# Moving the transposes of B and C from TensorE to the DMA from pair 4 on

## The chip, the cores and the metric

The kernel runs on one core of one Trainium2 chip. The metric is the time of one execution in microseconds on the device; the profile's span of the same execution is some 1.75 us shorter. Most repeated runs of one kernel agree within about 1%, and a run that is over 1.5% above the fastest of its kernel is called slow and left out of ratios.

## The reference, cut to what matters

A Mamba-2 style scan in chunks feeds a bilinear feed-forward layer: 4 batches, 8 heads, 768 positions, head dimension 32, state dimension 16; 3072 tokens of 256 features, 1536 hidden.

```python
for c in range(nc):                      # the reference uses chunks of 32; the kernel uses 128
    cum = np.cumsum(la, axis=-1)
    L = np.exp(cum[:, :, :, None] - cum[:, :, None, :]) * causal
    CB = np.einsum('bhin,bhjn->bhij', Cc, Bc)          # scores: contract over n
    y_intra = np.einsum('bhij,bhjd->bhid', CB * L, xc)
    y_inter = np.einsum('bhin,bhnd->bhid', Cc, state) * decay_to_i[:, :, :, None]
    ...                                                # state update
x = y.transpose(0, 2, 1, 3).reshape(B * S, H * D)
out = ((x @ w_a) * (x @ w_b)) @ w_out
```

The scores contract over n, so B and C, which arrive with positions on partitions, have to be transposed.

## The kernel before

A pair is two batches of one block of 128 positions; there are 12. A partition holds two neighbouring positions (i, r), r = 0 or 1. The loop from pair 4 on mixes the scan of pair p with the feed-forward of pairs p-1 and p-2:

```python
    def transposes(p, ps=None):
        ...
        for T_, src in ((TB, s["bm"]), (TC, s["cm"])):
            for r in range(2):
                nc.tensor.transpose(T_[:, r * 128 : (r + 1) * 128], src[:, r]..., ident)
        for e in range(2):                       # ScalarE, with the odd or even heads zeroed
            nc.scalar.activation(out=BT[:, e]..., in_=TB, func=AF.Copy, scale=par[:, e : e + 1])
        (nc.scalar.copy ...)(CT.rearrange("p t (i r) -> p r (t i)", r=2), TC...)   # natural order

    for p in range(4, NP):
        scores(p)                                # reads BT, CT of pair p
        if p + 1 < NP: scale(p + 1)              # GpSimd: B, C, x of the next pair
        if p + 2 < NP: load(p + 2)               # SyncE: six loads
        ...                                      # units (p - 1, 0..2) and masks
        out_half(p - 2, 0)                       # 12 matmuls, eviction, one store on SyncE
        go((p - 1, 3)); pull(p); pv(p); state(p)
        if p + 1 < NP: transposes(p + 1)
        out_half(p - 2, 1)
        ...
        go((p - 1, 4), (p - 1, 5))
```

Each engine runs its instructions in the written order; SyncE issues loads and stores in that order too.

## Time and profile before

| | before |
|---|---|
| time, median of 3 runs | 132.21 us (131.5 to 132.58) |
| span of the profiled run | 130.4 us |
| TensorE, VectorE, ScalarE, GpSimd busy | 93, 66, 57, 41% |
| scores of pair 4 start | 41.38 us |
| one pass of the loop, scores to scores | 9.38 us |

The last two rows come from the timeline of TensorE: the start of the first of 32 small matmuls (L279) marks each pass. Ends of matmuls are modelled and starts are not. The scores of pairs 4 to 6:

```profile
41.38 0.43 PE L279 MATMUL SC<-ct,bt 32*64 32x128 f16 x32
...
51.11 0.43 PE L279 MATMUL SC<-ct,bt 32*64 32x128 f16 x32
...
60.49 0.43 PE L279 MATMUL SC<-ct,bt 32*64 32x128 f16 x32
```

The stores of the kernel before, by tensor (durations of the issue in ns: least, median, most):

```profile
L454 SPq DMA_DIRECT2D out_dram<-osb x23: 332/338/570, 29.8 to 127.3; - x23
```

### The profile page before, as it was taken

What the parts mean: (1) busy time and instruction counts of PE and PEld (TensorE: products, weight loads), DVE (VectorE), ACT (ScalarE), POOL (GpSimd) and SP (SyncE); (2) the same over time, 40 slices, a digit from 0 to 9 for tenths busy, and PEclk for the clock granted to TensorE, in tenths of its full rate; (3) what the DMA queues carried; (4) which work ended last, traced back from release to release, by engine and by line L of the source; (5) the groups of instructions that cost most, each with busy time, mean ns of one, the idle gap of its engine ahead of it and who ended that gap; (6) DMA issues with size and microseconds to landing.
All of it is one profiled execution on the core that took longest, in us unless ns stands there. A gap on an engine that the chain in (4) does not pass through costs nothing.

```text
span 130.4 us, 4718 instructions
## 1 busy us (share of the span) xinstructions
PE 121.3 (93%) x1947; PEld 100.3 (77%) x1947; DVE 86.4 (66%) x163; ACT 74.9 (57%) x154; POOL 53.2 (41%) x72
## 2 busy tenths in 40 slices
PE   6959879988999999999999999999999999999980
PEld 2326758876888888888988888898888888888870
DVE  2676579592683975965966948948939829744440
ACT  3345576864647566576475576575486485464520
POOL 7787531943975808309219129037056000000000
PEclk9999999999999999999999999999999999999999
DMA  3999999047667452532623344514510110110102
GB/s 70 158 204 200 209 207 188 17 70 159 113 130 183 78 139 58 106 80 65 115 71 81 66 104 85 116 45 98 113 59 22 45 40 5 40 40 5 59 21 80
DMA packets 44805, 12.22 MB, mean 94 GB/s; under 512 B 38576, under 2 KB 44752, under 8 KB 44784
## 3 DMA queue, kind: packets, MB, share of 16 engines
q1 hardware_dynamic: 39264, 9.08, 33.1%
q0 software_dynamic: 3216, 2.36, 12.2%
q10 hardware_dynamic: 2304, 0.48, 1.8%
q8 instruction: 15, 0.25, 0.8%
q14 instruction: 6, 0.05, 0.2%
HBM read 11.13 MB, written 3.15 MB: 109 GB/s over the span
## 4 chain that ended last, share of the span: by engine, by line
PE 69%; DMA 19%; SPq 2%; DVE 2%; POOL 2%; ACT 1%; issue 1%; ACTq 1%; POOLq 0%; DVEq 0%
PE ops L437 22%; PE aps L420 19%; PE bps L420 19%; DMA Wo<-in_moe_w_out_dram 9%; DMA bn<-in_B_dram 5%; DMA cn<-in_C_dram 5%; PE SC L321 2%; PE SC L279 2%; PE SC L258 2%; SPq L122 2%; PE SC L355 2%; PE SC L338 1%; DVE hk L430 1%; POOL bm L240 1%; POOL cm L240 1%
## 5 line engine op out<-in xcount | busy, mean ns | idle before, releaser
L430 DVE TENSOR_TENSOR hk<-bps,asb 128x512 f16<-128x512 f32 x72 | 49.0, 687 | 25.0 <-ACT asb L429 24.1
L429 ACT COPY asb<-aps 128x512 f32<-128x512 f32 x72 | 41.9, 588 | 17.1 <-PE aps L420 15.6
L420 PE MATMUL bps<-X2T,Wb 128*128 128x256 f16 x288 | 43.2, 273 | 0.8 <-DMA Wb<-in_moe_w_b_dram 0.7
L420 PE MATMUL aps<-X2T,Wa 128*128 128x256 f16 x288 | 43.5, 273 | 0.0
L437 PE MATMUL ops<-Wo,hk 128*128 128x256 f16 x288 | 35.2, 273 | 0.0
L420 PEld LDWEIGHTS <-Wb 128*128 128x128 f16 x288 | 28.0, 98 | 4.7 <-DMA Wb<-in_moe_w_b_dram 1.0
L312 DVE TENSOR_TENSOR t<-SC,causal 128x512 f16<-128x512 f32 x45 | 29.4, 681 | 2.3 <-ACT tmp L309 2.0
L437 PEld LDWEIGHTS <-hk 128*128 128x128 f16 x288 | 27.7, 98 | 3.2
L420 PEld LDWEIGHTS <-Wa 128*128 128x128 f16 x288 | 26.8, 98 | 4.3 <-DVE X2T L379 0.3
L395 POOL TENSOR_TENSOR sbd<-U,maskbd 128x512 f16<-128x512 f32 x10 | 11.6, 1158 | 31.8 <-DVE U L391 31.7
L452 ACT ACTIVATE osb<-ops 128x256 f32<-128x256 f32 x23 | 8.8, 383 | 18.6 <-PE ops L437 18.6
L234 POOL TENSOR_SCALAR x<-xn 128x512 f16<-128x512 f32 x9 | 13.4, 1490 | 2.4 <-DMA xn<-in_x_dram 1.8
L367 ACT ACTIVATE X2T<-SC 128x512 f16<-128x512 f32 x11 | 6.6, 597 | 7.7 <-PE SC L338 6.7
L240 POOL TENSOR_TENSOR cm<-cn,fC 128x256 f16<-128x256 f32 x11 | 6.8, 619 | 7.4 <-DMA cn<-in_C_dram 7.3
L265 ACT ACTIVATE bt<-SC,ch 128x256 f16<-128x256 f16 x22 | 9.2, 471 | 0.7 <-PE SC L258 0.6
L391 DVE SCALAR_TENSOR_TENSOR U<-SC,G,gU 128x64 f32<-128x64 f32 x16 | 3.8, 280 | 6.4 <-ACT X2T L367 6.4
L240 POOL TENSOR_TENSOR bm<-bn,fB 128x256 f16<-128x256 f32 x11 | 6.9, 626 | 0.0
L279 PEld LDWEIGHTS <-bt 32*64 32x64 f16 x384 | 3.4, 104 | 3.2 <-issue 2.3
L279 PE MATMUL SC<-ct,bt 32*64 32x128 f16 x384 | 5.1, 220 | 0.7 <-ACT ct L266 0.4
L321 PEld LDWEIGHTS <-x 64*32 64x32 f16 x384 | 3.3, 90 | 3.2 <-ACT x L232 1.8
L186 PE MATMUL SC<-warm 128*128 128x512 f16 (+1 forms) x11 | 4.3, 545 | 1.2 <-DVE warm L149 1.2
L266 ACT COPY ct<-SC 128x256 f16<-128x256 f16 x11 | 5.0, 454 | 0.0
(59 smaller groups left out, 68.4 us busy)
## 6 DMA issues: line engine op xcount, KB each, us to landing
xn<-in_x_dram SPq DMA_DIRECT2D x23, 128.0 KB, 3.3
out_dram<-osb SPq DMA_DIRECT2D x23, 128.0 KB, 1.7
bn<-in_B_dram SPq DMA_DIRECT2D x23, 64.0 KB, 2.8
cn<-in_C_dram SPq DMA_DIRECT2D x22, 64.0 KB, 3.0
Wa<-in_moe_w_a_dram POOLq DMA_DIRECT2D x3, 256.0 KB, 6.3
Wb<-in_moe_w_b_dram POOLq DMA_DIRECT2D x3, 256.0 KB, 7.0
Wo<-in_moe_w_out_dram POOLq DMA_DIRECT2D x1, 768.0 KB, 11.9
cn<-in_C_dram ACTq DMA_DIRECT2D x2, 64.0 KB, 5.4
```

Source lines behind the costliest of these rows:

```text
L234: eng.tensor_scalar(xo, xi, XS, None, ALU.mult)
L240: eng.tensor_tensor(out=m_, in0=pair_in[p][which].rearrange("p h r n -> p r h n"), in1=f[:, blk, :, bp].unsqueeze(3).broadcast_to((128, 2, ...
L265: nc.scalar.activation(out=o_, in_=TB, func=AF.Copy, scale=par[:, e : e + 1])
L279: nc.tensor.matmul(SC[m][64 * bt : 64 * bt + 64, c0 : c0 + Q], BT[rows, e, r, bt], CT[rows, bt], start=True, stop=True, skip_group_check=True,
L312: nc.vector.tensor_tensor(out=o_, in0=i_, in1=c_, op=ALU.mult)
L367: nc.scalar.activation(out=X2T[:, p].rearrange("p u t q -> p t u q"), in_=SC1[:, :, 0:256].rearrange("p t (u q) -> p t u q", u=2), func=AF ...
L395: nc.gpsimd.tensor_tensor(out=Sbd.rearrange("p t (m c) -> p t m c", m=4), in0=U32[:, p].unsqueeze(2).broadcast_to((128, 2, 4, 2 * D)), in1 ...
L420: nc.tensor.matmul(ps[:, kk * 2 * Q : (kk + 1) * 2 * Q], W[:, f, k * 128 : (k + 1) * 128], X2T[:, p, f].rearrange("p t q -> p (t q)"), sta ...
L429: nc.scalar.copy(asb, a_ps)
L430: return lambda: nc.vector.tensor_tensor(out=s["hk"][:, 2 * k2 : 2 * k2 + 2, :].rearrange("p k q -> p (k q)"), in0=b_ps, in1=asb, op=ALU.mult)
L437: nc.tensor.matmul(o_ps[:, 0:d_model], hk[:, k, bt * Q : (bt + 1) * Q], Wo[:, k, :], start=(k == 0), stop=(k == NK - 1), skip_group_check= ...
L452: nc.scalar.activation(out=o_sb, in_=o_ps[:, 0:d_model], func=AF.Copy, scale=1.0 / (YS * YS))
```

## The change

The intent is to free TensorE of four transposes a pair and ScalarE of three evictions, with one DMA that transposes 128x768 elements from a tile of six planes (B of even heads, B of odd heads, C, each for r = 0 and 1; the zeros of the B planes are written once at the start). The DMA's output keeps queries in the order (r, i), so the causal mask changes, and each store of 128 rows becomes two of 64, each with every second row. Cut to its core:

```diff
+    bc = [big.tile([128, 6, H, N], f16, name=f"bc{i}") for i in range(2)]
+    bcT = [big.tile([128, 6, 2, 64], f16, name=f"bcT{i}") for i in range(2)]
...
+    DMA_T = 4
+    def scale_planes(p):                 # GpSimd: C planes once, B planes in two halves
+        ...
+    def dma_transposes(p):
+        o_ = bcT[p % 2]
+        nc.sync.dma_start(
+            o_.rearrange("p k t i -> p k (t i)"), bc[p % 2].rearrange("p k h n -> p (k h n)"), transpose=True
+        )
...
-            CT.rearrange("p t (i r) -> p r (t i)", r=2), TC.rearrange("p (r c) -> p r c", r=2)
+            CT.rearrange("p r t i -> p (r t i)"), TC
...
-        (q or nc.sync).dma_start(out[r0 : r0 + Q, :], o_sb)
+        dst = out[r0 : r0 + Q, :].rearrange("(i r) d -> r i d", r=2)
+        for r in range(2):
+            (q or (nc.sync, nc.sync))[r].dma_start(dst[r], o_sb[64 * r : 64 * r + 64])
...
     out_half(1, 1)
+    dma_transposes(4)
     pull(3)
     pv(3)
     state(3)
-    transposes(4)
...
         out_half(p - 2, 0)
+        if p + 1 < NP:
+            dma_transposes(p + 1)
         go((p - 1, 3))
         pull(p)
         pv(p)
         state(p)
-        if p + 1 < NP:
-            transposes(p + 1)
         out_half(p - 2, 1)
```

More of the change, by code (lines that the diff above doesn't have):

```diff
@@ L150 @@
     nc.vector.memset(zero, 0.0)
+    for t_ in bc:
+        nc.vector.memset(t_[:, 0:4].rearrange("p k h n -> p (k h n)").bitcast(u32), 0)
     nc.gpsimd.memset(sel, 1.0)
@@ L176 @@
     for bt in range(2):
-        v = causal[64 * bt : 64 * bt + 64]
+        v = causal[64 * bt : 64 * bt + 64].rearrange("p r (s i) -> p r s i", s=2)
         nc.gpsimd.affine_select(
-            out=v, in_=v, compare_op=ALU.is_ge, fill=0.0, base=0, pattern=[[-1, 2], [1, Q]], channel_multiplier=-2
+            out=v, in_=v, compare_op=ALU.is_ge, fill=0.0, base=0, pattern=[[-1, 2], [1, 2], [2, 64]], channel_multiplier=-2
         )
@@ L246, in scale_bc @@
         st.setdefault(p, {})[name] = m_
-    def scale(p):
+    DMA_T = 4
+    def scale_planes(p):
+        blk, bp = divmod(p, NBP)
+        bn, cn = (pair_in[p][w].rearrange("p h r n -> p r h n") for w in range(2))
+        c_ = bc[p % 2]
+        nc.gpsimd.tensor_tensor(
+            out=c_[:, 4:6], in0=cn, in1=fC[:, blk, :, bp].unsqueeze(3).broadcast_to((128, 2, H, N)), op=ALU.mult
+        )
+        for e in range(2):
+            nc.gpsimd.tensor_tensor(
+                out=c_[:, 2 * e : 2 * e + 2].rearrange("p r (m e) n -> p r m e n", e=2)[:, :, :, e],
+                in0=bn.rearrange("p r (m e) n -> p r m e n", e=2)[:, :, :, e],
+                in1=fB[:, blk, :, bp]
+                .rearrange("p r (m e) -> p r m e", e=2)[:, :, :, e]
+                .unsqueeze(3)
+                .broadcast_to((128, 2, H // 2, N)),
+                op=ALU.mult,
+            )
+    def dma_transposes(p):
+        o_ = bcT[p % 2]
+        nc.sync.dma_start(
+            o_.rearrange("p k t i -> p k (t i)"), bc[p % 2].rearrange("p k h n -> p (k h n)"), transpose=True
+        )
+        st[p]["BT"] = o_[:, 0:4].rearrange("p (e r) t i -> p e r t i", e=2)
+        st[p]["CT"] = o_[:, 4:6]
+    def scale(p):
+        if p >= DMA_T:
+            scale_planes(p)
+            scale_bc(p, 0, nc.gpsimd)
+            scale_x(p, nc.gpsimd)
+            return
         scale_bc(p, 1, nc.gpsimd)
@@ L261, in transposes @@
         BT = mid.tile([128, 2, 2, 2, 64], f16, name="bt", tag="bt")
-        CT = mid.tile([128, 2, Q], f16, name="ct", tag="ct")
+        CT = mid.tile([128, 2, 2, 64], f16, name="ct", tag="ct")
         for e in range(2):
@@ L281, in scores @@
                             BT[rows, e, r, bt],
-                            CT[rows, bt],
+                            CT[rows, :, bt],
                             start=True,
@@ L357, in pv @@
                         s["Sbd"][:, bt, u * 128 : u * 128 + 128],
-                        s["CT"][:, bt],
+                        s["CT"][:, :, bt],
                         start=(u == 0),
@@ L633 @@
         out_mm(NP - 1, bt, o[bt], range(NK - 2, NK))
-        out_store(NP - 1, bt, o[bt], on_dve=bt == 1, q=nc.scalar if bt == 0 else nc.sync)
+        out_store(NP - 1, bt, o[bt], on_dve=bt == 1, q=(nc.scalar, nc.sync))
 _INS = ['x', 'a', 'B', 'C', 'moe_w_a', 'moe_w_b', 'moe_w_out']
```

## The prediction

> **What bounds the kernel now.** I read the page first: busy shares, then the chain of work that ended last, then the groups.
>
> ```profile
> PE 121.3 (93%) x1947; PEld 100.3 (77%) x1947; DVE 86.4 (66%) x163; ACT 74.9 (57%) x154; POOL 53.2 (41%) x72
> ...
> PEclk9999999999999999999999999999999999999999
> ...
> PE 69%; DMA 19%; SPq 2%; DVE 2%; POOL 2%; ACT 1%; issue 1%; ACTq 1%; POOLq 0%; DVEq 0%
> ...
> L265 ACT ACTIVATE bt<-SC,ch 128x256 f16<-128x256 f16 x22 | 9.2, 471 | 0.7 <-PE SC L258 0.6
> L258 PE MATMUL SC<-ident,bm 128*128 128x128 f16 x22 | 3.1, 224 | 0.6 <-POOL bm L240 0.6
> ...
> L266 ACT COPY ct<-SC 128x256 f16<-128x256 f16 x11 | 5.0, 454 | 0.0
> ```
>
> TensorE is busy 93% of 130.4 us, at full granted clock everywhere, and carries 69% of the chain; the 19% of DMA lie before 32 us, while weights and first inputs arrive. ScalarE, whose evictions the change removes (L265, L266), is busy 57% and names no wait of TensorE in the steady part. I then took the busy time by stretches, one loop pass each: the pass from 60.56 to 69.95 us has TensorE busy 9.39 of 9.39 us. So from about 45 us a pass costs what TensorE's instructions cost, and nothing else.
>
> What an instruction is worth there is not its duration, because matmuls overlap. The timeline of TensorE in that pass shows start times:
>
> ```profile
> 63.48 1.47 PE L437 MATMUL ops<-Wo,hk 128*128 128x256 f16 x12
> ...
> 66.49 0.29 PE L258 MATMUL SC<-ident,bm 128*128 128x128 f16 x2
> 66.61 0.27 PE L258 MATMUL SC<-ident,cm 128*128 128x128 f16 x2
> 66.73 1.47 PE L437 MATMUL ops<-Wo,hk 128*128 128x256 f16 x12
> ...
> 69.88 0.32 PE L279 MATMUL SC<-ct,bt 32*64 32x128 f16 x16
> ```
>
> The four transposes of a pair occupy 66.49 to 66.73: 0.24 us, not 4 x 224 ns. The scores of the next pair (L279, their first reader) start at 69.88, over 3 us later.
>
> The other queue that matters is SyncE's, because every new DMA goes onto it in program order. Its timeline around the place where the first DMA transpose is put in:
>
> ```profile
> 34.62 0.57 SPq L454 DMA_DIRECT2D out_dram<-osb  x1
> 35.28 1.80 SPq L122 DMA_DIRECT2D bn<-in_B_dram  x2
> 37.13 1.30 SPq L122 DMA_DIRECT2D cn<-in_C_dram  x2
> 38.48 1.31 SPq L122 DMA_DIRECT2D xn<-in_x_dram  x2
> 39.90 1.04 SPq L454 DMA_DIRECT2D out_dram<-osb  x2
> ```
>
> From 25 to 46 us this queue has no pause: a load takes some 0.65 us to issue, a store 0.34 to 0.57. The first of the two stores at 39.90 had its data since 36.88 (ScalarE's eviction started at 36.50 and took 0.38). SyncE is late here by 3 us already. In the steady passes it has room: the loads of the pass end at 64.10, and the store at 65.40 waits for its eviction.
>
> **What the Trainium skill says.** (1) "VectorE: DVE Perf Modes", section "The three transpose paths": a 128x128 two-byte transpose takes 390 ns on TensorE and 1309 ns by the DMA crossbar. The trace agrees that TensorE's is cheap (224 ns long, 0.06 us of its time); it has no DMA transpose. (2) "DMA: Bandwidth & Descriptors", section "Latency and other measured facts": a DMA transpose moved 261 GB/s in one kernel. No run here shows it yet. (3) The same page, section "Anatomy of one DMA — SWDGE (gpsimd) path": DMA engines don't wait on semaphores, the wait is on the issuing sequencer. The trace agrees for SyncE: its stores waited 46.5 us in all for ScalarE's evictions, and what stood behind them waited too. (4) "TensorE: Matmul & The Clock Gate", section "Part 1: The HAM clock gate": an idle window of about 3.4 us halves the array's clock, and as long a busy one restores it. The trace before has no such gap after its start, and its clock row is 9 throughout.
>
> **The change, part by part.**
>
> Removed, for pairs 4 to 11: four TensorE transposes each. Seven of the eight lie in full passes: 7 x 0.24 = 1.7 us off the path. Removed on ScalarE: 2 x 0.47 + 0.45 = 1.4 us a pair, off the path, except at pair 4, where the chain runs through L265 at 40.46 and later through VectorE; TensorE lost about 0.4 us there (in its timeline a group of four bps matmuls starts at 44.28, 0.73 us after the group ahead of it, where 0.44 is the rule, and another small gap lies at 41.8). That may come back, so at most 2.1 us in all, or 1.6%. A gain of 2% (2.6 us) is more than there is.
>
> Added on GpSimd: planes need C once (0.62 us), B in two halves (0.35 us each, my estimate from half of 626 ns plus a fixed part), and bm again for the state: 0.7 us a pair more. GpSimd is idle 5.1 us of a pass; off the path. The memsets of VectorE at the start (2 x 0.27 us, as that of `warm`, which has the same size) fall into its wait of 1.57 us for `a`.
>
> Added on SyncE: 24 stores become 48 of half the size, about 0.4 us more issue each, and eight transposes of 128x768, six blocks of 128x128.
>
> How long from the issue of such a transpose to its landing? Call it L. Estimate from the skill: 1309 ns for the first block, plus five blocks of 32 KB at 261 GB/s, 5 x 0.125 = 0.6 us: 1.9 us. In this trace a store of 128 KB lands 1.7 us after issue, a load of 128 KB 3.3 us. The transpose queues behind two stores on the same engines, and its issue may be longer than a store's. I take L = 2.8 us, and hold 2 to 6 possible.
>
> Steady passes: the transpose of the next pair stands after the store of L437's first half. Its eviction ends 65.37, two stores take 0.7 to 0.8, so it starts at 66.15; the scores would now start at 69.88 - 0.24 = 69.64. That leaves 3.5 us. With L = 2.8 it is hidden by 0.7 us. Each us over 3.5 is paid seven times.
>
> Pair 4: here it stands behind load 5 and four half stores. Two earlier stores that also became two push the queue back by about 0.8 us, so load 5 ends near 40.5 in place of 39.8; four stores at 0.45 us: the transpose starts at about 42.4 and lands at 42.4 + 2.8 = 45.2. The scores of pair 4 started at 41.38 before, and TensorE has nothing else to run, since its order is fixed. So it idles about 4 us, a delay against before of 45.2 - 41.4 = 3.8 us. Nothing wins it back, because everything after is bound by TensorE.
>
> End: the last two half stores are issued one behind the other on two queues, 0.37 us more on ScalarE's, with half the bytes: +0.1 us.
>
> Sum: -1.7 - 0.4 + 3.8 + 0.1 = +1.8 us. The idle stretch of about 4 us is just past the 3.4 us of the clock gate: at a chance of one in three some 3.4 us at half clock, costing 1.7 us, worth 0.6 on average. And L in excess of 3.5 at a chance of a third. So 132.2 + 1.8 + 0.6 gives 134.6, and with the tail of L I name 134.9.
>
> **The rivals.** First: L is over the 3.5 us of the steady passes. For it: crossbar writes of 32 bytes to each partition could cost a packet each; q1's packets took 33.1% x 16 x 130.4 / 39264 = 17.6 ns, and 384 such per engine would be 6.8 us. Against it: 261 GB/s of the skill. With L = 4.5, pair 4 loses 5.5 and each of seven passes 1.0: 132.2 - 2.1 + 5.5 + 7 + 0.1, some 143 us. TensorE would wait for the DMA in every pass. Second: L near 2 and no clock loss: pair 4 loses 3.0, in all +1.0: 133.2, called the same. Third: the stall at pair 4 doesn't come, because SyncE is quicker there than I think; then -1.6% stays, 130.2. Against it: SyncE issued the last of the stores before that place at 40.4 to 40.9 already without the extra ones, and the scores were due at 41.38. Fourth: SyncE becomes the bound in the passes: 6 loads at 0.65, 4 stores at 0.4 and a transpose's issue of up to 2.5 make 8.0 of 9.15 us, so not quite.
>
> **Range and chances.** The low end, 133.0, is L = 2 with a short stall; the high end, 144, is L about 4.6. Faster by over 2% exceeds the gain there is: 0.03. Within 2% (up to 134.85) needs L under 3.4 and a warm clock: 0.45. Slower: 0.52.
>
> **What would show it.** In the profile after: TensorE's transposes (L258, bm and cm into SC) fall from 22 to 6 of each kind, ScalarE's busy time by about 11 us, the pass from scores to scores goes from 9.39 to 9.15 us. A single TensorE wait of 3 to 5 us for the transposed tile stands near 41 to 46 us, with SyncE issuing four stores before it. If the waits are spread over all passes, L is over 3.5 us and the first rival holds. If the clock row dips near 45 us, the gate closed. If no wait stands at pair 4, my reading of SyncE's order is wrong and the time is below 132.

## The result, and the profile after

The changed kernel took 144.24 us (143.87 to 146.18, 4 runs) where the kernel before took 132.08 in the same rounds. The ratio is 1.091 (95% interval 1.085 to 1.098). Ratios here are the mean time of one kernel's fast runs over that of the other's of the same rounds, so they are not quite the ratio of the medians. The prediction, 134.9 us in a range of 133.0 to 144.0, was wrong: the direction was right, and the size was missed by more than a factor of four (12 us against 2.7).

The page of the kernel after, busy shares, the clock row and the chain of work that ended last:

```profile
PE 122.2 (86%) x1915; PEld 100.0 (70%) x1915; DVE 87.7 (61%) x165; ACT 66.8 (47%) x130; POOL 59.3 (42%) x88
...
PEclk9999999999995559999999999999999999999998
...
PE 50%; DMA 24%; SPq 14%; ACT 3%; DVE 2%; issue 2%; POOL 1%; POOLq 0%; ACTq 0%
```

TensorE's share of the chain fell from 69 to 50%, SyncE's queue (SPq) rose from 2 to 14%, and the clock row has three slices of 5 (3.6 us each, in part idle). ScalarE lost 8 us of busy time, which bought nothing.

SyncE's timeline around the first DMA transpose, to be held against the five lines of before:

```profile
35.80 1.22 SPq L496 DMA_DIRECT2D out_dram<-osb  x2
37.12 1.35 SPq L127 DMA_DIRECT2D bn<-in_B_dram  x2
38.52 1.31 SPq L127 DMA_DIRECT2D cn<-in_C_dram  x2
39.87 2.25 SPq L127 DMA_DIRECT2D xn<-in_x_dram  x2
42.22 2.49 SPq L496 DMA_DIRECT2D out_dram<-osb  x4
44.82 1.31 SPq L277 DMA_TRANSPOSE bcT<-bc  x1
```

The queue is packed as before, and the transpose starts at 44.82 us. Its planes had been ready since about 37.9 us: GpSimd starts the two halves of B at 37.08, and they take 0.77 together. So the transpose waited nearly 7 us for its place in line, and for nothing else.

TensorE's timeline (the bracket is the idle time before, and what ended it):

```profile
47.68 0.65 PE L319 MATMUL SC<-bcT 32*64 32x128 f16 x32 [6.99 <-DMA bcT<-bc]
48.27 1.03 PE L460 MATMUL aps<-X2T,Wa 128*128 128x256 f16 x4
...
60.28 0.43 PE L319 MATMUL SC<-bcT 32*64 32x128 f16 x32 [0.88 <-DMA bcT<-bc]
60.64 0.61 PE L460 MATMUL aps<-X2T,Wa 128*128 128x256 f16 x4
...
69.72 0.43 PE L319 MATMUL SC<-bcT 32*64 32x128 f16 x32 [0.21 <-DMA bcT<-bc]
```

There is one wait of 6.99 us at pair 4. After it the same four matmuls take 1.03 us in place of 0.61. Shorter waits follow in the later passes: 0.88, 0.21, 0.58, 0, 1.33, 0.61 and 0.70 us. Busy time by stretches shows the clock (the column after POOL):

```profile
47.68:53.16 5.48, 5.48 (x57) 3.92 (x57) 3.59 (x6) 1.58 (x3) 0.00 (x0) 0.52 0.51 95
60.28:69.72 9.44, 9.23 (x157) 7.92 (x157) 6.31 (x12) 4.85 (x9) 4.24 (x6) 1.00 0.59 105
```

In the first of them TensorE ran at a granted clock of 0.52, and took 5.48 us from the scores to the first output matmul; with the clock at 1.00 (60.28 to 63.27) that takes 2.99.

The stores and the transposes of the kernel after, from the same view by line (issue in ns: least, median, most; then us from issue to landing of the transposes):

```profile
L496 SPq DMA_DIRECT2D out_dram<-osb x46: 466/580/760, 29.1 to 139.2; - x46
```

```profile
L277 SPq DMA_TRANSPOSE bcT<-bc x8: 1236/1574/2582, 44.8 to 115.2; - x8
...
DMA to landing us min/median/max: 2.8/3.4/4.3
```

A store of 64 rows with every second row takes 0.58 us to issue, where one of 128 neighbouring rows took 0.34. Two halves cost 1.16 us of SyncE in place of 0.34.

Where the 12.4 us of span come from, by start times of TensorE:

| stretch | before | after | difference |
|---|---|---|---|
| start to scores of pair 4 | 41.38 | 47.68 | +6.30 |
| pass 4 (scores 4 to scores 5) | 9.73 | 12.60 | +2.87 |
| passes 5 to 10, together | 56.14 | 58.58 | +2.44 |
| scores 11 to the last output matmuls | 16.77 | 16.77 | 0 |
| from there to the end | 6.38 | 7.17 | +0.79 |

The rows sum to 12.40. Pass 4 is the half clock (2.49), the wait of 0.88, less 0.24 for the transposes and less some 0.35 that this pass had lost before to ScalarE's chain. In passes 5 to 10 the waits listed above sum to 3.4 us, against the 6 x 0.24 = 1.4 won. The 0.4 that this leaves open is some 0.07 us in each of the five passes with a wait, over the recorded wait itself (9.44 less 0.21 is 9.23, where the pass without a wait takes 9.16).

### The profile page after: what moved, and what is told of

Same layout as the page of the kernel before. It is cut to its first block, busy times and chain, and to the rows that moved or that the text cites. A ratio compares the mean times of both kernels' runs of the same rounds, so it can differ in the third digit from the quotient of the medians.

```text
span 142.8 us, 4683 instructions
## 1 busy us (share of the span) xinstructions
PE 122.2 (86%) x1915; PEld 100.0 (70%) x1915; DVE 87.7 (61%) x165; ACT 66.8 (47%) x130; POOL 59.3 (42%) x88
## 4 chain that ended last, share of the span: by engine, by line
PE 50%; DMA 24%; SPq 14%; ACT 3%; DVE 2%; issue 2%; POOL 1%; POOLq 0%; ACTq 0%
PE aps L460 15%; DMA bcT<-bc 15%; PE bps L460 13%; PE ops L477 13%; SPq L127 10%; DMA cn<-in_C_dram 5%; DMA xn<-in_x_dram 4%; SPq L496 4%; PE SC L319 3%; PE SC L361 2%; ACT asb L469 1%; DVE hk L470 1%; PE fps L217 1%; PE SC L395 1%; DVE t L352 1%
## 5 line engine op out<-in xcount | busy, mean ns | idle before, releaser
L460 PE MATMUL aps<-X2T,Wa 128*128 128x256 f16 x288 | 44.9, 279 | 0.0
L460 PE MATMUL bps<-X2T,Wb 128*128 128x256 f16 x288 | 44.4, 278 | 0.3 <-DMA Wb<-in_moe_w_b_dram 0.3
L460 PEld LDWEIGHTS <-Wb 128*128 128x128 f16 x288 | 28.7, 100 | 4.4 <-DMA Wb<-in_moe_w_b_dram 0.5
L460 PEld LDWEIGHTS <-Wa 128*128 128x128 f16 x288 | 27.4, 100 | 4.9 <-DVE X2T L419 0.3
L319 PE MATMUL SC<-bcT 32*64 32x128 f16 x256 | 3.7, 231 | 11.3 <-DMA bcT<-bc 11.3
L319 PEld LDWEIGHTS <-bcT 32*64 32x64 f16 x256 | 2.3, 110 | 13.5 <-DMA bcT<-bc 13.5
L261 POOL TENSOR_TENSOR bc<-cn,fC 128x256 f16<-128x256 f32 x8 | 5.0, 619 | 2.9 <-DMA cn<-in_C_dram 2.9
L265 POOL TENSOR_TENSOR bc<-bn,fB 128x128 f16<-128x128 f32 x16 | 6.1, 405 | 0.0
L350 POOL TENSOR_TENSOR t<-tmp,causal 128x512 f16<-128x512 f32 x3 | 3.5, 1154 | 4.5 <-ACT tmp L349 4.5
```

The source lines that it names most:

```text
L319: nc.tensor.matmul(SC[m][64 * bt : 64 * bt + 64, c0 : c0 + Q], BT[rows, e, r, bt], CT[rows, :, bt], start=True, stop=True, skip_group_chec ...
L460: nc.tensor.matmul(ps[:, kk * 2 * Q : (kk + 1) * 2 * Q], W[:, f, k * 128 : (k + 1) * 128], X2T[:, p, f].rearrange("p t q -> p (t q)"), sta ...
```

## The experiments

After the result my theory (A) was: the transpose of pair 4 stands too far back in SyncE's queue (6.3 us), the wait throws TensorE to half clock (2.5), the later ones land too late by their place in the pass, and the two-part stores lengthen the tail. Rivals: the order of queries, the doubled stores and the extra work of GpSimd cost by themselves (B), or a DMA transpose is too slow wherever it is put (C). Four runs of the first round came on one chip, with before at 132.69 us (median of 7).

**Only the layout.** All transposes stay on TensorE; query order and two-part stores as changed.

```diff
-    DMA_T = 4
+    DMA_T = 12
-    dma_transposes(4)
+    transposes(4)                        # after state(3), as before; likewise in the loop
```

> Only the query order and the two-part stores stay; all transposes are TensorE's again. If the loss of the change comes from where and when the DMA transposes are issued (theory A), only the tail of +0.8 us remains: 133.0 us, between 132.3 and 133.6, with no wait over 1 us in the passes. If the order and the doubled stores cost time by themselves, by SyncE's issue or by contention (rival B), 135 us or more. TensorE's scores of pair 4 should start near 41.4 us under A.

Measured: 133.1 us (ratio 1.008, interval 0.9995 to 1.016), no wait of TensorE that the layout made, scores of pair 4 at 41.27 us, passes of 9.38. The span from the scores of pair 11 to the end was 23.94 us against 23.15: all of the loss is the tail's 0.79. From the timelines of TensorE and of SyncE:

```profile
41.27 0.43 PE L319 MATMUL SC<-ct,bt 32*64 32x128 f16 x32
...
42.77 2.50 SPq L496 DMA_DIRECT2D out_dram<-osb  x4
```

So the order of queries and the doubled stores, two parts of rival B, fall as costs of their own. The third part, GpSimd's extra work, is not tested here, since this kernel builds no planes; it is in the last two kernels below, which beat their control all the same. SyncE's queue was just as late here, its four half stores starting at 42.77 us, but nobody waited for them. That is the point: lateness of a store was free here, and lateness of a transpose in the same line is not.

**The first transpose ahead of the loads of pair 5.**

```diff
     scale(4)
+    dma_transposes(4)
     load(5)
...
     out_half(1, 1)
-    dma_transposes(4)
```

> The change as it is, but the transpose of pair 4 is issued ahead of the six loads of pair 5 instead of behind them and four half stores. Theory A: it lands near 41 us, TensorE's wait of 7.0 us goes below 1 us, the clock row stays 9, and the time falls by about 6.3 + 2.7 = 9 us to 135.2 (134.3 to 136.5). Rival C (the transpose itself is too slow for any place, or other waits take over): 140 us or more.

Measured: 141.33 us, a ratio of 1.069: only 3 of the expected 9 us came back, so the theory as I had put it fell. The profiled run was slow, so its times of day are not compared, but its waits show what happened (TensorE's timeline):

```profile
43.51 0.43 PE L319 MATMUL SC<-bcT 32*64 32x128 f16 x32 [2.13 <-DMA bcT<-bc]
...
57.34 0.65 PE L319 MATMUL SC<-bcT 32*64 32x128 f16 x32 [4.60 <-DMA bcT<-bc]
```

The stall at pair 4 shrank to 2.13 us, and one of 4.60 us arose at pair 5. Load 5, four half stores and load 6 were pushed behind, and the next transpose stood behind them. Two things of this run blur the picture: SyncE stood idle for 1.8 us ahead of the first transpose, because its planes were ready only at 38.9 us, and that transpose took 4.5 us to land. My reading was that it is not the place of one DMA: SyncE's queue as a whole is behind, from 25 us to beyond 50 us, and moving one item forward moves the wait to the next. This became theory A2, the backlog.

**Earlier in every pass.** The transpose goes ahead of the first half's stores, right behind the loads.

```diff
             load(p + 2)
+        if p + 1 < NP:
+            dma_transposes(p + 1)
...
         out_half(p - 2, 0)
-        if p + 1 < NP:
-            dma_transposes(p + 1)
```

> The change as it is, but in the passes the transpose of the next pair is issued right behind the loads, ahead of the first half's stores, some 2 us earlier. Theory A: the waits for the transposed tile in the passes after the first (0.2 to 1.3 us each) vanish, each pass from scores to scores takes 9.15 us, and the sum falls by about 4.6 us to 139.7 (138.8 to 140.6); the 7 us at pair 4 stay. Rival C: landing stretches just as much because the transpose then runs beside the loads; waits stay and the time is within 1 us of 144.2.

Measured: 140.58 us (ratio 1.063), 3.7 us under the change where 4.6 were expected. Its passes from pair 5 on became 9.16 us apart or less, with one exception, a wait of 1.15 us at pair 9, where the transpose took 5.2 us to land. The waits in the passes are thus a matter of place, and rival C falls for all but that one.

**TensorE kept busy in the stall.** Thirty idle matmuls ahead of the scores of pair 4.

```diff
     for p in range(4, NP):
+        if p == 4:
+            warmup(30, SC[3])
         scores(p)
```

> The change as it is, with 30 idle matmuls of 512 columns (6.5 us at full clock) put before the scores of pair 4, in the 7 us where TensorE waits. If the half clock after that wait costs what the start times say (5.48 us from 47.68 to 53.16 for work of 3.0 us), the time falls by 2.3 to 2.6 us to 141.8, with the clock row at 9. If those matmuls were slow for another reason, the time stays at 144.2 or rises.

Measured: 140.66 us (ratio 1.064): 3.7 us less than the change, although work was added. Its clock row is 9 throughout. The half clock was thus a real cost. It was expected at 2.3 to 2.6 us; the rest of the 3.7 may lie in shorter waits of the later passes (2.2 us in sum in its profile, against 4.3), and I have not separated that.

**From pair 6 on**, at the change's own place in the pass, and **from pair 6 on and early in the pass**. These and the next two shared a chip, with before at 132.67 us.

```diff
-    DMA_T = 4
+    DMA_T = 6
-    dma_transposes(4)
+    transposes(4)                        # after state(3), and in the loop while p + 1 < 6
-        if p + 1 < NP:
+        if DMA_T <= p + 1 < NP:          # second kernel: this goes behind load(p + 2)
             dma_transposes(p + 1)
```

> The change, but by DMA only from pair 6 on, issued at the same place in the pass. The run that moved pair 4's transpose ahead showed the stall turn up again at pair 5 (4.6 us): SyncE's queue as a whole is behind until about 55 us. Theory A2 (that backlog is the cause of the first stall): with six transposes that start after it, TensorE never waits over 2 us and the clock row stays 9; what is left are short waits in the passes (about 0.5 us each, six times), 1.2 at pair 6 and the tail of 0.8, less 6 x 0.24: about 136 us (134.5 to 137.5). If the first transpose stalls wherever it is (rival: a cost of the first use), a wait of 4 us or more stands at pair 6 and the time is 139 or more.

> From pair 6 on, and in the pass right behind the loads. Theory A2: all six transposes are hidden, TensorE's passes go to 9.15 us, and only the tail of 0.8 us stands against 6 x 0.24 = 1.4 us: 0 to 1 us under the kernel before, 132.2 where before reads 132.7. Rival: waits on the transposed tile of over 0.5 us stay, 134 or more.

Measured: 135.76 us for the first (two of four runs were slow; the fast ones took 134.68 in the mean, ratio 1.017), with the longest wait on the transposed tile 1.2 us and the clock at 9; 132.91 for the second (ratio 0.9996, interval 0.993 to 1.006), where two waits of 0.61 and 0.90 us were left. Once the queue has caught up there is no long stall, so it is not a cost of first use. With the place mended too, nothing is lost and nothing gained: what TensorE saves, six times 0.24 us, goes to the two waits and the longer tail (1.5 and 0.4 us in the profiled run, the slowest of the three fast ones).

**Single stores, natural order by a strided read.** The change at its own places, but the scores' moving operand is read as (i, r), and stores are whole again.

```diff
-                            CT[rows, :, bt],
+                            CT[rows, :, bt].rearrange("p r i -> p i r"),
...                                       # the same for Sbd; mask and store as before
```

> The change with DMA transposes at the places it has them, from pair 4 on, but queries in their natural order (the scores' moving operand is read in the order (i, r), two strides) and so one store of 128 rows as before. Theory A2: SyncE has four issues of about 0.6 us less before pair 4's transpose and one pair of them less in each pass, so the first stall shrinks from 7.0 to about 4.5 us, the transposes in the passes start 0.8 us earlier and are mostly hidden, the tail's 0.8 goes: about 138 us (135.5 to 139). If doubled stores do not matter for the queue, 143 or more. If the strided read costs TensorE time, its scores take over 0.43 us a pair.

Measured: 143.16 us (ratio 1.078), against an expected 138. The queue did what the theory says: the transpose started at 41.74 us and the wait was 3.87 us in place of 6.99. But the read cost most of what the stores had won: a kernel below has single stores without this read, at a ratio of 1.041, so that the read took back 4.9 us of 6.7 (groups by line; the two numbers behind the bar are busy us and mean ns of one):

```profile
L319 PE MATMUL SC<-bcT 32*64 32x128 f16 x256 | 5.5, 285 | 4.9 <-DMA bcT<-bc 4.9
L395 PE MATMUL SC<-bcT,sbd 128*128 128x128 f16 x32 | 5.2, 284 | 0.0
```

A scores matmul became 280 ns long (median) in place of 214, and the 32 of a pair took 0.63 us from start to start in place of 0.36. "SBUF — State Buffer" in the Trainium skill, section "Door 1: The DMA port swizzle", says that accesses which cross to another 16-byte line each time pay a penalty. Neighbouring queries here lie 256 bytes apart. The trace agrees in that the read is slower (280 ns against 214); that this is the reason no run shows. This cost is what the two-part store of the change was there to avoid.

**All three mends with that read**: from pair 6 on, early in the pass, natural order by the strided read.

```diff
-    DMA_T = 4
+    DMA_T = 6
...                                       # dma_transposes behind load(p + 2), as in the early run
-                            CT[rows, :, bt],
+                            CT[rows, :, bt].rearrange("p r i -> p i r"),
...                                       # mask, state and store as in the run above
```

> All three mends: from pair 6 on, issued right behind the loads, natural order and single stores. Theory A2: no waits, passes of 9.15 us from pair 6 on, no longer tail: 1.4 us under the kernel before (131.3 where before reads 132.7), the gain that the removal of TensorE's transposes was worth. Rival: the gain does not show, because other waits fill it; within 0.3 us of before.

Measured: 135.54 us (ratio 1.019). There was not one wait on the transposed tile, and passes were 9.69 us: 9.15 + 0.54, where the 0.54 is the strided read of scores and state. The expectation missed that cost, since this run was sent off together with the one that found it.

**The order undone at the eviction.** Queries stay in the order (r, i) up to ScalarE's eviction of the scan's result, which writes them back in natural order; matmuls read contiguous rows and stores are single. Four kernels, with before at 132.36 us: the change's own places from pair 4 on, a control without DMA transposes, and the early place from pair 6 and from pair 5 on.

```diff
-            out=X2T[:, p].rearrange("p u t q -> p t u q"),
-            in_=SC1[:, :, 0:256].rearrange("p t (u q) -> p t u q", u=2),
+            out=X2T[:, p].rearrange("p t u (i r) -> p (t u) r i", r=2),
+            in_=SC1[:, :, 0:256].rearrange("p t (g i) -> p t g i", g=4),
...
-                        X2T[:, p, f].rearrange("p t q -> p (t q)"),
+                        X2T[:, p, :, f],
...
-        for r in range(2):
-            (q or (nc.sync, nc.sync))[r].dma_start(dst[r], o_sb[64 * r : 64 * r + 64])
+        (q or nc.sync).dma_start(out[r0 : r0 + Q, :], o_sb)
```

> The change at its own places (from pair 4 on, behind the first half's store), with nothing altered but the order undone at the eviction and so single stores. The run with the strided read showed the first transpose at 41.7 us and a stall of 3.9 us, but paid 0.54 us a pass for that read. Here: the same stall of about 4 us, passes of 9.15 us but for waits of about 0.3, no longer tail: 137 us (135.5 to 138.5). So some 7 of the 12 us of the change come from the doubled stores in SyncE's queue. If 141 or more, they do not.

Measured: 138.19 us (ratio 1.041, against the change's 1.091). The first wait was 3.24 us. SyncE's timeline of this kernel, at the place of the first transpose:

```profile
38.73 1.31 SPq L127 DMA_DIRECT2D xn<-in_x_dram  x2
40.14 1.04 SPq L495 DMA_DIRECT2D out_dram<-osb  x2
41.27 1.90 SPq L277 DMA_TRANSPOSE bcT<-bc  x1
```

The two stores ahead of the transpose take 1.04 us in place of 2.49 for four halves, the last loads are not stretched, and the transpose starts 3.5 us earlier than in the change. By the difference of the ratios, 0.05 of 132, the doubled stores and what they caused cost 6.7 us, over half of the 12; the change's own places from pair 4 on still cost 5.4 with them gone. Part of that is the clock again (TensorE's timeline):

```profile
44.85 0.66 PE L319 MATMUL SC<-bcT 32*64 32x128 f16 x32 [3.24 <-DMA bcT<-bc]
45.44 1.03 PE L461 MATMUL aps<-X2T,Wa 128*128 128x256 f16 x4
```

From 44.85 to 47.84 us the granted clock was 0.52, and the work up to the first output matmul took 4.30 us in place of 3.00: 1.3 us lost after a wait of only 3.24.

> Control for the two: the same order up to the eviction and the same single stores, but all transposes by TensorE. It should be the kernel before within 0.4 us (132.7), with passes of 9.39 us and scores of 0.36 us a pair. If it is faster than that, part of the gain of the other two is the order's and not the transposes'.

Measured: 132.44 us (ratio 0.999): undoing the order at the eviction costs and wins nothing. ScalarE's eviction grew from 597 to 745 ns, which lies beside other work.

> As the run from pair 5 on, but from pair 6. Theory A2: 6 x 0.24 = 1.4 us under the kernel before, 131.3 where before reads 132.7, with no waits. Rival (what is removed from TensorE comes back elsewhere): within 0.4 us of before.

Measured: 130.68 us (129.78 to 131.49), ratio 0.988 (interval 0.982 to 0.993). No TensorE wait on the transposed tile. TensorE's timeline, two neighbouring passes:

```profile
60.31 0.43 PE L319 MATMUL SC<-bcT 32*64 32x128 f16 x32
...
69.47 0.43 PE L319 MATMUL SC<-bcT 32*64 32x128 f16 x32
```

The pass is 9.16 us, and there is no bracket of idle time. SyncE's timeline in the pass before the first of them:

```profile
53.08 1.27 SPq L127 DMA_DIRECT2D xn<-in_x_dram  x2
54.45 1.31 SPq L277 DMA_TRANSPOSE bcT<-bc  x1
56.06 3.36 SPq L495 DMA_DIRECT2D out_dram<-osb  x2
```

The transpose starts at 54.45, 5.9 us ahead of its reader, and it is now the stores that stand behind it.

> DMA transposes from pair 5 on, issued right behind the loads of the pass; queries in the order (r, i) only up to ScalarE's eviction into X2T, which writes them back in natural order, so the matmuls read contiguous rows and the store is one of 128 rows. Theory A2 (backlog of SyncE's queue, long issue of half stores, no cost of the transposes themselves where they are hidden): no waits on the transposed tile over 0.3 us, passes of 9.15 us, no longer tail: 7 x 0.24 = 1.7 us under the kernel before, 131.0 where before reads 132.7. Rival: pair 5 still meets the backlog, a wait of 1 us or more stands there, 132 or more.

Measured: 130.66 us (129.73 to 131.18 over five fast runs), ratio 0.986 (interval 0.980 to 0.992). A sixth run, the profiled one, took 203 us at a mean clock of 0.56; from that slow run nothing is concluded, so that the waits of this kernel are not known. Both kernels beat the one before and the change: the gain of 1.2 to 1.4% is what removing TensorE's transposes, with ScalarE's evictions of them, is worth.

## Why the prediction was wrong, point by point

- *TensorE is the bound, and four transposes are worth 0.24 us a pair.* Right. Where all else was mended, the pass fell from 9.38 to 9.16 us, and from pair 6 on the kernel won 1.6 us against its control (132.29 against 130.67, means of fast runs) where 1.4 was expected. ScalarE's busy time fell by 8.1 us, not by about 11: the durations of its evictions sum to 10.6 us less, but they had overlapped one another (two in a row take 0.83 us, not twice 0.47). This was off the path in either case.
- *A gain of 2% is more than there is.* Right; the best kernel found wins 1.4%.
- *L, from issue to landing, is 2.8 us.* Right for the first transpose (2.82), low for most of the later ones: median 3.4, up to 4.3. The estimate from the Trainium skill's 1309 ns and 261 GB/s, 1.9 us, was never reached: 2.7 us was the least in any kernel. The reason given for a long L, a packet for every 32 bytes and so 6144 for a transpose, is not what happened: queue q1 moved 45664 packets in the kernel that undoes the order at the eviction from pair 4 on, and 39264 in its control, which is 800 for each of the eight transposes.
- *"Pair 4: ... the transpose starts at about 42.4."* This is the step that failed most. It stood behind the items I had named, but started at 44.82. From the first split stores to the end of load 5 SyncE took 13.07 us (29.05 to 42.12) in place of 9.95. Half stores account for 1.3 of the 3.1 extra: a pair of them took 1.2 us, not twice 0.45. Loads of x whose issue stretched account for 2.1 (2.48 and 2.25 us, where before each took 1.31), less 0.3 by other loads. Then the four half stores took 2.49 us, not 1.8. That the doubled stores are behind it is shown by the single-store run, in which the transpose started at 41.27; why the issue of loads stretches, the trace does not say.
- *The stall is about 4 us, and the half clock a chance of one in three.* The mechanism was right, and both sizes were off. The stall was 6.99 us. The half clock cost 2.5 us by start times; the run with idle matmuls won 3.7, which need not all be the clock's. The chance was too low even for a stall of the predicted length: waits of 3.24 and 3.87 us, in the single-store and the strided kernel, were followed by half clock too (1.3 and 1.7 us lost), and so was each wait of over 3 us on the transposed tile in the kept traces, five of five. Together, by start times, they make 8.8 us (6.3 + 2.5), where the prediction had allowed 4.4 (3.8 + 0.6).
- *Steady passes leave 3.5 us for L, hidden by 0.7.* Wrong. The transpose started 6.19 us after the scores, not 5.66 (66.15 less 60.49), because the two half stores ahead of it take 1.16 us. That leaves 2.96 us for an L of 2.8 to 4.3. Passes 5 to 10 lost 2.4 us where 1.4 was to be won. The first rival, L over the window, was the right name with a wrong number: it was the window that shrank more than L that grew.
- *SyncE as the bound, "not quite".* In the steady passes that held. Between 25 and some 50 us it was the bound, and the run with the first transpose moved ahead points to it, the wait coming back one pair later; that the two kernels with a start at pair 6 have no long stall agrees.
- *Tail +0.1 us.* It was +0.79. The two half stores on ScalarE's queue took 1.39 us to issue and on SyncE's 1.11, where single ones took 0.37 and 0.33; both queues issue at once and each half takes longer than a whole.

Not tried were single stores with the early place from pair 4 on, and transposes issued from another engine's queue, away from SyncE's line. Left open are the stretched issues, and the transpose of pair 9, which landed late in most kernels (4.3 us after its issue in the change, 5.2 in the run early in the pass), but not in the two with single stores, the early place and a start at pair 6 (3.5 at most).

## What to carry to other kernels

Before you put a transfer that someone waits for onto an in-order queue, add up what stands ahead of it there, with the issue times of the new forms and not of the old ones: the stores here were microseconds late at no cost, the input of a waiting engine was not. Put the awaited transfer directly behind its own inputs, ahead of the stores. When moving one item forward only moves the wait to the next, the queue itself is the bound, and the remedy is fewer or cheaper issues, or a later start of the scheme.

## What the Trainium skill lacked or had wrong

- "DMA: Bandwidth & Descriptors" has no issue time of a DMA transpose measured on this chip (only sequencer cycles that a vendor document gives for "previous generations"), and its 261 GB/s says little at this size: 128x768 two-byte elements from SBUF to SBUF took 1.21 to 2.58 us of SyncE to issue and 2.7 to 5.2 us to land. Nor does it say that stores of half the size can take longer to issue: 0.58 us for 64 rows (every second row of the output) against 0.34 for 128 neighbouring ones; whether the step or the halving does it was not separated. Its advice against two transfers to disjoint partition halves (section "Rules for kernel authors") holds here, through the issue time: 1.16 us for two halves in place of 0.34.
- "VectorE: DVE Perf Modes", "The three transpose paths", gives 1309 ns for 128x128 by DMA without saying whether issue and landing are in it. For six such blocks 2.7 us was the least seen.
- "TensorE: Matmul & The Clock Gate" has nothing on the access pattern of the moving operand, which at a step of 256 bytes made a scores matmul 280 ns long in place of 214; only the SBUF page has a mechanism that fits. What it says of the clock gate, in "Part 1: The HAM clock gate", half clock after an idle window of about 3.4 us, agrees: 6.99 us idle brought the granted clock to 0.52. So did 3.24 us, a little under that window; as ends of matmuls are modelled, this is no contradiction.
